# Sketched attention and a gated network on one core: weight columns regrouped for narrowing, the first batch's q handled in pieces, row transfers merged

## The chip, the cores and the metric

The kernel runs on one core of a Trainium2 chip. TensorE (PE in the profile) multiplies matrices, VectorE (DVE), ScalarE (ACT) and GpSimd (POOL) do elementwise work, SyncE (SP) issues most of the transfers, and 16 DMA engines move data between HBM and the on-chip memories: SBUF, and PSUM, where TensorE writes. Each engine runs its own instructions in the order in which they were written, and waits for others by semaphores. The metric is the time of one execution on the device, in microseconds. Lower is better.

## What is computed

```
phi(x) = outer product of (S1 x) and (S2 x), 8 x 8 = 64 features     # S1, S2: 8 x 32
kv  = phi(k)^T v ;  z = sum over the sequence of phi(k)
num = phi(q) kv  ;  den = phi(q) z + 1e-6
attn = num / den                       # 4 batches, 4 heads, 1088 positions, 32 per head
x = attn as (4 * 1088, 128)            # the heads side by side
out = (sigmoid(x w_gate) * (x w_val)) w_out     # w_gate, w_val: 128 x 1536, w_out: 1536 x 128
```

All of it is float32, but S1, S2 and the three weights arrive as float64. [...]the kernel reads them as pairs of 32-bit words and builds float32 values from the pair on the chip. The text calls this narrowing.

## The kernel before

**The network.** The 4352 tokens are cut into eight chunks of 512 and one of 256, and the 1536 hidden columns into NJ = 12 blocks of 128, numbered j. `w1` (line 345) does one wave: x times the gate block and x times the value block into a PSUM tile `wave`, a sigmoid on ScalarE into `sg` (line 365), and, by the `glu` that it leaves behind, the product `g` on VectorE (line 381). `w2` (line 307) multiplies a `g` with the block of w_out and accumulates in `moeout`, which lies in one of two PSUM banks, acc0 for even chunks and acc1 for odd ones. `slot(group, waves)` (line 395) runs a piece of other work and then so many waves; within each wave it first does the pending `glu`, then a `w2` that lies two waves back, then `w1`. The engines' order is exactly this order of calls.

**The attention.** For batch 0 it runs ahead of the network and delivers the tokens in two pieces: 512 tokens (n = 0) before the first wave, 576 tokens (n = 1) during the first chunk. `turn_q` (line 430) transposes q on VectorE, `qcomp` (line 593) multiplies it by the sketch (`cqps`) and copies the result to `cq`, `spread` (line 617) writes `cq` to a scratch tensor `dq` in HBM and reads it back with every row repeated, into `qp` and `bq`, and `qmult` (line 653) multiplies the two to the features of q. `dn` (line 835) makes the denominators (`dps`), the numerators (`nps`), and divides them into `xT`. Batches 1 to 3 are worked on between waves by the loop at line 1035.

**Narrowing.** `narrow` (line 83) is a generator with four steps. Step 0 clamps the high words into `cap` on GpSimd (line 97) and scales the low words into `tail` on ScalarE (line 101). Step 1 shifts and masks `cap` into `head` in two instructions on VectorE (lines 105 and 109). Step 2 squares `cap` on ScalarE (line 117) and adds `tail` to `head` on GpSimd (line 118). Step 3 multiplies `head` with a test on the square on VectorE, into the weight tile `w_sb` (line 127). The square goes to a PSUM bank if one is named, else back over `cap`.

The blocks 0 and 1 are narrowed by `narrow_01` in three parts: gate and value of block 0, gate and value of block 1, and w_out of both (256 columns each). From block 2 on `narrow_w(j, step)` takes gate, value and w_out of block j together (384 columns), one block per wave of the first chunk, in the lines that `w1` runs when `ci == 0`:

```
            if 0 < j0 < NJ - 2:
                narrow_w(j0 + 1, 3)
            narrow_w(j0 + 2, 1)
            narrow_w(j0 + 2, 2)
```

Their squares lie in bank acc1, except for blocks 10 and 11, which have none. The `dps` of piece n = 1 lies in acc1 as well.

**The order of the first chunk** is written out by hand: wave 0; wave 1; `turn_q(0, 1)` between waves 1 and 2; wave 2; then `q01` (`qcomp` and `spread` for piece 1) and waves 3 to 8; `qmult(0, 1)` in one instruction; `load_kq(1)`, which loads k and q of batch 1 into the buffer that `bq` held; wave 9; `part(0, 1)`, that is the pending `glu` and `dn(0, 1)`, with the last step of block 11 inside its division; waves 10 and 11.

**The transfers.** SP issues in this order: S1, S2, the first part of q, gate and value of block 0, v, gate and value of block 1, w_out of blocks 0 and 1, the rest of q, and then pair by pair gate, value and w_out of two blocks. `spread` makes four row transfers for each piece: for each half c of the partitions, one into `qp` and one into `bq`, 64 partitions each.

Of the kernel before, what the change touches and what calls it, by code (L numbers as in the profile page):

```python
# [9 lines left out]
I32 = mybir.dt.int32  # L10
# [10 lines left out]
def kernel(  # L21
# [32 lines left out]
    sbA = ctx.enter_context(tc.tile_pool(name="sbA", bufs=2))  # L54
    raw = ctx.enter_context(tc.tile_pool(name="raw", bufs=NJ // 2))
    sbN = ctx.enter_context(tc.tile_pool(name="sbN", bufs=1))
# [26 lines left out]
    def narrow(out, bits, eng, bank=None, copies=None):  # L83
# [7 lines left out]
        def tmp(dt, tag, bufs):  # L91
# [15 lines left out]
            op0=ALU.logical_shift_left, op1=ALU.bitwise_and,  # L107
        )
        nc.vector.scalar_tensor_tensor(  # L109
            out=head, in0=cap, scalar=-0x40000000, in1=head, op0=ALU.bitwise_and, op1=ALU.bitwise_or  # L110
# [33 lines left out]

    w_sb = const.tile([P, 3, NJ, P], F32, tag="w_sb", name="w_sb")
    w_in = {}

    def load_w_in(j0, j1):
        cs = slice(j0 * P, j1 * P)
        n, jj = divmod(j0, 2)  # L150
        if wide and jj == 0:
            w_in[n] = raw.tile([P, 3, 2, P, 2], I32, tag="w_in", name="w_in")
        for i, src in enumerate((moe_w_gate, moe_w_val)):
            if wide:
                nc.sync.dma_start(
                    out=w_in[n][:, i, jj : jj + j1 - j0].rearrange("p j m w -> p (j m w)"),
                    in_=src[:, cs].bitcast(I32),
                )
            else:
                nc.sync.dma_start(  # L160
                    out=w_sb[:, i, j0:j1].rearrange("p j m -> p (j m)"), in_=src[:, cs]
                )

    def load_w_out(n):
        j0, j1 = 2 * n, 2 * n + 2
        cs = slice(j0 * P, j1 * P)
        src = moe_w_out[cs, :].bitcast(I32) if wide else moe_w_out[cs, :]
        nc.sync.dma_start(
            out=w_in[n][:, 2].rearrange("p j m w -> p j (m w)") if wide else w_sb[:, 2, j0:j1],
            in_=src.rearrange("(j p) m -> p j m", p=P),  # L170
        )

    narrowing = {}

    def narrow_w(j, step):
        if not 0 <= j < NJ:
            return
        n, jj = divmod(j, 2)
        if wide:
            if step == 0:  # L180
                narrowing[j] = narrow(
                    w_sb[:, :, j, :], w_in[n][:, :, jj], nc.gpsimd, "acc1" if j < NJ - 2 else None
                )
            next(narrowing[j])


    def narrow_01(part, step):
        if wide:
            if step == 0:
                i = (slice(0, 2), part) if part < 2 else (2, slice(0, 2))  # L190
                narrowing["01", part] = narrow(
                    w_sb[:, i[0], i[1]],
                    w_in[0][:, i[0], i[1]],
                    nc.gpsimd,
                    "acc0" if part else "acc1",
                )
            next(narrowing["01", part])

# [46 lines left out]
    load_w_in(1, 2)  # L245
    load_w_out(0)
    load_rows(q, 0, q_t[0], ((T0, T, nc.sync),))
    for n in range(1, NJ // 2):
        load_w_in(2 * n, 2 * n + 2)
        load_w_out(n)  # L250

# [55 lines left out]
    def w2(ci, j0, jn, g):  # L307
# [4 lines left out]
        for jj in range(jn):  # L312
            j = j0 + jj
            nc.tensor.matmul(  # L314
                out=moe["acc"][:, :tw],
                lhsT=w_sb[:, 2, j, :],
                rhs=g[:, jj, :tw],
                start=(j == 0),
                stop=(j == NJ - 1),
            )  # L320
        if j0 + jn == NJ:
# [6 lines left out]
            while c < t0 + tw:  # L328
# [14 lines left out]
                c += n * 32  # L343

    def w1():

# [7 lines left out]
        for o in range(0, tw, tp):  # L354
            for which in range(2):
                for jj in range(jn):
                    nc.tensor.matmul(  # L357
                        out=wv[:, which, jj * tw + o : jj * tw + o + tp],
                        lhsT=w_sb[:, which, j0 + jj, :],
                        rhs=xT[:, t0 + o : t0 + o + tp],  # L360
                        start=True,
                        stop=True,
                    )
        sg = sbG.tile([P, TCH], F32, tag="sg", name="sg", bufs=3)
        nc.scalar.activation(out=sg, in_=wv[:, 0], func=ACTF.Sigmoid)  # L365
        if ci == 0:
            if j0 == 1:
                narrow_01(2, 3)
            if 0 < j0 < NJ - 2:
                narrow_w(j0 + 1, 3)  # L370
            narrow_w(j0 + 2, 1)
            narrow_w(j0 + 2, 2)
            if j0 < 3:
                narrow_w(j0 + 3, 0)
            if j0 > 1:
                narrow_w(j0 + 4, 0)

# [51 lines left out]

    def turn_q(b, n):  # L430
        if b >= B:
            return
        if n == 0:
            qT_of[b] = sbA.tile([P, TP, 2, 32], F32, tag="qT", name="qT", bufs=1)
        t0, tn = q_chk[n]
        nc.vector.transpose(  # L436
            out=qT_of[b][:, t0 : t0 + tn].rearrange("p t c s -> p (t c s)"),
# [179 lines left out]
    def spread(b, ns, cq, put, get):  # L617
# [3 lines left out]
        for n in ns:  # L621
            for c in range(2):
                for i, t in enumerate((QP[b], BQ[b])):
                    d0 = d[64 * n + 32 * c + 2 * i, 0]
                    rows = [[8 * W1, R], [0, R]] if i == 0 else [[0, R], [8 * W1, R]]
                    get.dma_start(  # L626
                        out=t[64 * c : 64 * c + 64, n * H * W1 : (n + 1) * H * W1],
                        in_=bass.AP(
                            tensor=d0.tensor, offset=d0.offset, ap=rows + [[1, H * W1]]
                        ),  # L630
                    )

        if len(ns) < 2:
# [18 lines left out]

    def qmult(b, n):
        q0 = half(QP[b], n)
        nc.vector.tensor_tensor(out=q0, in0=q0, in1=half(BQ[b], n), op=MUL)  # L655

# [38 lines left out]
    def kvd(b):  # L695
        KVD[b] = sbA.tile([P, 2, 2, F], F32, tag="kvd", name="kvd")
        k0 = KVZ[b][:, : 2 * F]
# [209 lines left out]
    if wide:  # L907
        steps = narrow(s4, s_in, nc.vector, copies=4)
        for _ in range(3):
            next(steps)  # L910
# [54 lines left out]
    for pi in range(2):  # L965
        outer(0, pi, NJK - 1, NJK, eng=nc.gpsimd)
    for part in range(2):
        narrow_01(part, 0)
    spread_z()
# [8 lines left out]
    def rest(turn, rc, dT):  # L978
# [7 lines left out]
        kvd(0)  # L986
        narrow_01(0, 1)
        narrow_01(0, 2)
        ndt(0)
# [4 lines left out]
    def head1():  # L994
        narrow_01(1, 1)
        narrow_01(0, 3)
        narrow_01(1, 2)
        narrow_01(2, 0)
        narrow_w(2, 0)

    divide((0, 4), (4, 8), between=head1)
    narrow_01(1, 3)
    narrow_01(2, 1)
    narrow_01(2, 2)

# [11 lines left out]

    def part(b, n, between=None):
        glu()
        dn(b, n)(between=between)  # L1020

# [3 lines left out]

    slot(None, 1)
    turn_q(0, 1)
    slot(None, 1)
    slot(q01, 6)
    qmult(0, 1)  # L1030
    load_kq(1)
    slot(None, 1)
    slot(lambda: part(0, 1, lambda: narrow_w(NJ - 1, 3)), 2)
    v_t[1] = load_v(1)
    for b in range(1, B):
        more = b + 1 < B
        wn = 1 if b == 1 else 2
        turn_k(b)
        turn_q(b, 0)
        slot(None, wn)  # L1040
        turn_q(b, 1)
        slot(lambda: begin(b), 1)
        for pi in range(2):
# [50 lines left out]
```

## Time and profile before

| | |
|---|---|
| median of 6 runs | 304.6 us (304.46 to 305.35) |
| the profiled execution | 304.56 us, of which 302.8 us from the first to the last instruction (the span) |
| clock that was granted to TensorE | 0.997 of full |
| weight DMAs: gate, value | 256 KB each for two blocks, 5.8 and 4.8 us from issue to landing |
| weight DMAs: w_out | 256 KB for two blocks, 7.1 us |
| row DMAs of batches 1 to 3, `qp` and `bq` | 288 KB each, 9.7 and 10.0 us |

The numbers after an "x" are counts. A line of a timeline reads: start from the beginning of the span, length, engine, line of the code, operation, what is written and what is read, shape, and in brackets how long the engine stood idle ahead of it and who ended that. "PEld" is TensorE's loading of weights, which runs beside its products. A matrix product of float32 appears as two records for each instruction.

### The profile page before, as it was taken

To read this page: it belongs to the slowest core of one execution; us is meant where nothing else is said; L and a number is where in the kernel's file an instruction comes from. 1 tells how busy PE (TensorE), PEld (TensorE's weight loads), DVE (VectorE), ACT (ScalarE), POOL (GpSimd) and SP (SyncE) were. 2 spreads that over 40 slices of the span, in tenths; PEclk is the share of its full clock that TensorE was granted. 3 is DMA by queue.
4 is the path that set the end of the run, shared out by engine and by line. 5 is a ranking of instruction groups with operands and counts; after the bars stand their busy time and mean duration, and the time that the engine had idled before them with its cause. 6 is when DMAs were issued, how large, how long until landed. Compare 5 with 4: busy or idle time off the path is not lost.

```text
span 302.8 us, 3657 instructions
## 1 busy us (share of the span) xinstructions
PE 296.0 (98%) x1363; PEld 136.3 (45%) x1363; DVE 154.6 (51%) x268; ACT 80.7 (27%) x150; POOL 36.3 (12%) x68
## 2 busy tenths in 40 slices
PE   8899999999999999999999999999999999999995
PEld 3444433443444444434444444444444444444683
DVE  6997788774645554364465541744232223222331
ACT  3556532222122222221222222221222222222220
POOL 1465540610000400000002300000000000000000
PEclk9999999999999999999999999999999999999998
DMA  7993440797201493360013990200010000100011
GB/s 218 350 343 74 124 141 8 169 211 182 93 10 24 110 216 69 72 191 1 0 20 79 173 156 4 36 2 0 0 26 8 0 0 10 27 0 0 8 30 17
DMA packets 31410, 24.24 MB, mean 80 GB/s; under 512 B 21344, under 2 KB 26592, under 8 KB 31392
## 3 DMA queue, kind: packets, MB, share of 16 engines
q1 hardware_dynamic: 27024, 16.15, 20.5%
q0 software_dynamic: 3456, 7.09, 12.1%
q10 hardware_dynamic: 912, 0.77, 0.9%
q8 instruction: 11, 0.18, 0.3%
q14 instruction: 7, 0.06, 0.1%
HBM read 20.73 MB, written 3.26 MB: 79 GB/s over the span
## 4 chain that ended last, share of the span: by engine, by line
PE 84%; DMA 7%; DVE 4%; POOL 3%; issue 1%; SPq 1%; ACT 0%; POOLq 0%
PE wave L357 52%; PE moeout L314 27%; DMA v<-in_v_dram 3%; POOL head L118 3%; DMA w_in<-in_moe_w_out_dram 2%; DMA w_in<-in_moe_w_gate_dram 2%; DVE w_sb L127 1%; DVE head L109 1%; PE kvz L677 1%; PE nps L864 1%; DVE head L105 1%; PE kps L456 1%; PE cqps L602 0%; PE denj L798 0%; PE deni L812 0%
## 5 line engine op out<-in xcount | busy, mean ns | idle before, releaser
L357 PE MATMUL wave<-xT,w_sb 128*128 128x512 f32 (+1 forms) x436 | 191.7, 565 | 0.1
L381 DVE TENSOR_TENSOR g<-wave,sg 128x512 f32<-128x512 f32 x102 | 70.3, 690 | 133.4 <-ACT sg L365 133.2
L357 PEld LDWEIGHTS wave<-xT,w_sb 128*128 128x128 f32 x436 | 82.6, 190 | 93.6 <-issue 86.4
L365 ACT ACTIVATE sg<-wave 128x512 f32<-128x512 f32 x102 | 60.9, 597 | 199.0 <-PE wave L357 193.1
L314 PE MATMUL moeout<-g,w_sb 128*128 128x512 f32 (+1 forms) x216 | 105.8, 577 | 0.3 <-DVE w_sb L127 0.3
L314 PEld LDWEIGHTS moeout<-g,w_sb 128*128 128x128 f32 x216 | 39.3, 190 | 44.0 <-issue 37.4
L626 POOL DMA_DIRECT2D qp<-dq x12 | 7.1, 590 | 108.7 <-DMA dq<-cq 68.7
L118 POOL TENSOR_TENSOR head<-head,tail 128x384 int32<-128x384 int32 (+2 forms) x14 | 13.3, 953 | 18.2 <-DVE head L109 15.1
L535 DVE TENSOR_TENSOR kp<-kab 128x1152 f32<-128x1152 f32 (+2 forms) x10 | 10.5, 1070 | 0.0
L655 DVE TENSOR_TENSOR qp<-qp,bq 128x1152 f32<-128x1152 f32 (+1 forms) x7 | 9.0, 1288 | 1.2 <-DMA bq<-dq 1.2
L109 DVE SCALAR_TENSOR_TENSOR head<-cap,head 128x384 int32<-128x384 int32 (+2 forms) x14 | 7.5, 535 | 0.5
L127 DVE SCALAR_TENSOR_TENSOR w_sb<-square,head 128x384 f32<-128x384 f32 (+1 forms) x11 | 5.7, 519 | 3.9 <-POOL head L118 3.9
L258 PE MATMUL warm<-const-float32-1.0 128*128 128x512 f32 (+1 forms) x12 | 6.6, 666 | 0.8 <-PEq L1078 0.8
L626 POOL DMA_DIRECT2D bq<-dq x12 | 6.9, 576 | 0.4 <-issue 0.2
L324 DVE STREAM_TRANSPOSE o_sb<-moeout 128x512 f32<-128x512 f32 (+1 forms) x9 | 6.1, 678 | 1.4 <-PE moeout L314 1.3
L101 ACT ACTIVATE tail<-w_in 128x384 int32<-128x384 uint32 (+1 forms) x13 | 6.6, 522 | 0.5 <-DMA w_in<-in_moe_w_gate_dram 0.5
L97 POOL TENSOR_SCALAR cap<-w_in 128x384 f32<-128x384 f32 (+1 forms) x13 | 6.4, 500 | 0.0
L897 DVE TENSOR_TENSOR xT<-nps,rb 128x576 f32<-128x576 f32 (+2 forms) x9 | 5.9, 661 | 0.7
L864 PE MATMUL nps<-qp,nd 64*32 64x256 f32 (+1 forms) x128 | 5.5, 401 | 0.4 <-ACT nd L741 0.4
L436 DVE STREAM_TRANSPOSE qT<-kq 128x512 f32<-128x512 f32 (+1 forms) x8 | 5.8, 719 | 0.0
L117 ACT ACTIVATE square<-cap 128x384 f32<-128x384 f32 (+1 forms) x11 | 5.1, 464 | 1.8 <-DVE w_sb L127 1.7
L425 DVE STREAM_TRANSPOSE kT<-kq 128x1088 f32<-128x1088 f32 (+2 forms) x5 | 5.3, 1070 | 0.0
(89 smaller groups left out, 85.2 us busy)
## 6 DMA issues: line engine op xcount, KB each, us to landing
qp<-dq POOLq DMA_DIRECT2D x12, 288.0 KB, 9.7
bq<-dq POOLq DMA_DIRECT2D x12, 288.0 KB, 10.0
v<-in_v_dram SPq DMA_DIRECT2D x16, 144.0 KB, 6.4
kq<-in_k_dram SPq DMA_DIRECT2D x3, 544.0 KB, 4.2
kq<-in_q_dram SPq DMA_DIRECT2D x3, 544.0 KB, 5.1
w_in<-in_moe_w_out_dram SPq DMA_DIRECT2D x6, 256.0 KB, 7.1
w_in<-in_moe_w_gate_dram SPq DMA_DIRECT2D x5, 256.0 KB, 5.8
w_in<-in_moe_w_val_dram SPq DMA_DIRECT2D x5, 256.0 KB, 4.8
```

Of the source, the lines that this page charges most:

```text
L101: nc.scalar.activation(out=tail, in_=lo, func=ACTF.Copy, scale=2.0**-29)
L109: nc.vector.scalar_tensor_tensor(out=head, in0=cap, scalar=-0x40000000, in1=head, op0=ALU.bitwise_and, op1=ALU.bitwise_or)
L118: nc.gpsimd.tensor_tensor(out=head, in0=head, in1=tail, op=ALU.add)
L127: nc.vector.scalar_tensor_tensor(out=out, in0=square, scalar=1.265625 * 2.0**-30, in1=head, op0=ALU.is_ge, op1=MUL)
L314: nc.tensor.matmul(out=moe["acc"][:, :tw], lhsT=w_sb[:, 2, j, :], rhs=g[:, jj, :tw], start=(j == 0), stop=(j == NJ - 1),)
L357: nc.tensor.matmul(out=wv[:, which, jj * tw + o : jj * tw + o + tp], lhsT=w_sb[:, which, j0 + jj, :], rhs=xT[:, t0 + o : t0 + o + tp], sta ...
L365: nc.scalar.activation(out=sg, in_=wv[:, 0], func=ACTF.Sigmoid)
L381: nc.vector.tensor_tensor(out=g, in0=wv[:, 1], in1=sg, op=MUL)
L535: eng.tensor_tensor(out=KP[b][:, pi, j0:j1].rearrange("p j m (i l) -> p (j m) i l", i=R), in0=bass.AP(tensor=a0.tensor, offset=a0.offset, ...
L626: get.dma_start(out=t[64 * c : 64 * c + 64, n * H * W1 : (n + 1) * H * W1], in_=bass.AP(tensor=d0.tensor, offset=d0.offset, ap=rows + [[1, ...
L655: nc.vector.tensor_tensor(out=q0, in0=q0, in1=half(BQ[b], n), op=MUL)
L864: nc.tensor.matmul(out=t[32 * h : 32 * h + 32, c, :w], lhsT=ND[b][rows, 32 * h : 32 * h + 32], rhs=half(QP[b], n)[rows, 2 * (h % 2) + h // ...
```

## The change

Five things change.

1. Gate, value and w_out are grouped differently. Alone are now: gate and value of blocks 0, 1 and 2 (256 columns each), and w_out of blocks 0 and 1 (128 columns each). From block 3 on, gate and value of block j go together with w_out of block j - 1 (384 columns), and w_out of block 11 comes alone at the end (128 columns). The weight tile and the tiles of raw words are laid out to suit; the DMAs of w_out are 0, then 1, then 2, then 3 and 4, and so on to 11 alone, one DMA more than before. All squares of blocks 3 to 11 lie in acc1.
2. `narrow` has five steps: the two VectorE instructions of step 1 are steps 1 and 2.
3. q of batch 0, piece 1: its transpose comes in two instructions (320 and 256 wide) in waves 2 and 3, its product in three (288, 576 and 288 wide) in waves 8, 9 and 10. `q01` runs after wave 3 instead of wave 2, and `part(0, 1)` after wave 10 instead of wave 9. The work of batches 1 to 3 shifts by one wave against the network with it; batch 1 has a wave between the transposes of k and of q.
4. The row transfers into `qp` are one for both halves (128 partitions); those into `bq` stay two. This holds for all batches.
5. `kvd` has one buffer instead of two.

```diff
     def narrow(out, bits, eng, bank=None, copies=None):
...
+        yield
         nc.vector.scalar_tensor_tensor(
             out=head, in0=cap, scalar=-0x40000000, in1=head, op0=ALU.bitwise_and, op1=ALU.bitwise_or
         )
...
+    for j in range(NJ if wide else 0):
+        bits = w_in[j // 2][:, :, j % 2]
+        if j < 3:
+            at = slice(j, j + NJ + 1, NJ)
+            places["gv", j] = at, bits[:, :2], f"acc{1 - j % 2}"
+        else:
+            at = slice(j, j + 2 * NJ + 1, NJ)
+            places[j] = at, bits, "acc1"
+    if wide:
+        for j, bank in enumerate(("acc0", None)):
+            places["out", j] = (
+                slice(2 * NJ + 1 + j, 2 * NJ + 2 + j), w_in[j][:, 2, 1 - j : 2 - j], bank
+            )
+        places[NJ] = slice(3 * NJ, 3 * NJ + 1), w_in[NJ // 2][:, 0], None
...
     load_w_in(1, 2)
-    load_w_out(0)
+    load_w_out(0, 1)
+    load_w_out(1, 2)
     load_rows(q, 0, q_t[0], ((T0, T, nc.sync),))
...
     def w1():
...
         if ci == 0:
...
+            if j0 == 0:
+                narrow_w(("gv", 2), 1, 2, 3)
+                narrow_w(("out", 0), 4)
+                narrow_w(3, 0)
+            elif j0 == 1:
+                narrow_w(("gv", 2), 4)
+                narrow_w(("out", 1), 1, 2, 3)
+                narrow_w(3, 1, 2)
+                narrow_w(("out", 1), 4)
+                narrow_w(3, 3)
+                narrow_w(4, 0)
+            else:
+                if j0 in between:
+                    between[j0]()
+                narrow_w(j0 + 1, 4)
+                narrow_w(j0 + 2, 1, 2, 3)
+                if j0 <= 6:
+                    narrow_w(j0 + 3, 0)
+                if j0 >= 6:
+                    narrow_w(j0 + 4, 0)
...
     def spread(b, ns, cq, put, get):
...
-            for c in range(2):
-                for i, t in enumerate((QP[b], BQ[b])):
+            for i, t in enumerate((QP[b], BQ[b])):
+                for c in (0, 1) if i else (0,):
                     d0 = d[64 * n + 32 * c + 2 * i, 0]
-                    rows = [[8 * W1, R], [0, R]] if i == 0 else [[0, R], [8 * W1, R]]
+                    rows = [[0, R], [8 * W1, R]] if i else [[8 * W1, 2 * R], [0, R]]
                     get.dma_start(
-                        out=t[64 * c : 64 * c + 64, n * H * W1 : (n + 1) * H * W1],
+                        out=t[64 * c : 64 * c + 64 if i else P, n * H * W1 : (n + 1) * H * W1],
...
-    slot(None, 1)
-    turn_q(0, 1)
-    slot(None, 1)
-    slot(q01, 6)
-    qmult(0, 1)
+    between.update(
+        {
+            2: lambda: turn_q(0, 1, 0, 5),
+            3: lambda: turn_q(0, 1, 5),
+            8: lambda: qmult(0, 1, 0, 1),
+            9: lambda: qmult(0, 1, 1, 3),
+            10: lambda: qmult(0, 1, 3),
+        }
+    )
+    slot(None, 3)
+    slot(q01, 7)
     load_kq(1)
-    slot(None, 1)
-    slot(lambda: part(0, 1, lambda: narrow_w(NJ - 1, 3)), 2)
+    slot(lambda: part(0, 1), 1)
...
     for b in range(1, B):
...
+        glu()
         turn_k(b)
+        if b == 1:
+            slot(None, 1)
+            glu()
         turn_q(b, 0)
-        slot(None, wn)
+        if b > 1:
+            slot(None, wn)
         turn_q(b, 1)
+        if b == 1:
+            slot(None, wn)
         slot(lambda: begin(b), 1)
```

The head of the program calls the same steps by their new names: of gate and value 0 and 1 in the same places as before, then of w_out 0 alone where w_out of both blocks stood.

## The prediction

> **What bounds the kernel now.** I read the busy table first, then the chain of waits, then the timelines of TensorE, VectorE and GpSimd from 8 to 52 us, then the table of stretches for the transfers.
>
> ```profile
> PE 296.0 (98%) x1363; PEld 136.3 (45%) x1363; DVE 154.6 (51%) x268; ACT 80.7 (27%) x150; POOL 36.3 (12%) x68
> ```
>
> TensorE is the bound, and from 46 us on nothing interrupts it: in the chain of waits a wave (two products of 512 columns) takes 1.72 us and a `moeout` product 0.86 us, back to back to the end. Only the first 46 us have gaps. TensorE's timeline (start, length, engine, line):
>
> ```profile
> 15.16 3.71 PE L357 MATMUL wave<-xT,w_sb 128*128 128x256 f32 x12
> 19.21 1.12 PE L314 MATMUL moeout<-g,w_sb 128*128 128x512 f32 x2 [0.34 <-DVE w_sb L127]
> 20.17 1.88 PE L357 MATMUL wave<-xT,w_sb 128*128 128x512 f32 x4
> 21.98 0.69 PE L602 MATMUL cqps<-qT,skq 64*32 64x288 f32 x8
> ...
> 39.01 1.88 PE L357 MATMUL wave<-xT,w_sb 128*128 128x512 f32 x4
> 40.94 0.69 PE L844 MATMUL dps<-qp,zb 128*32 128x288 f32 x8
> ...
> 43.17 1.88 PE L357 MATMUL wave<-xT,w_sb 128*128 128x512 f32 x4
> 44.88 1.02 PE L314 MATMUL moeout<-g,w_sb 128*128 128x512 f32 x2
> 46.00 1.98 PE L357 MATMUL wave<-xT,w_sb 128*128 128x512 f32 x4
> ```
>
> The modelled end lies 0.16 behind the true one (1.88 against 1.72), so the first two waves end at 18.71. The gaps: 0.50 before 19.21, 0.10 before 20.17, 0.09 before 21.98, 0.21 before 40.94, 0.26 before 46.00. With 0.1 for the wave that follows a stall (46.00 to the next product at 47.82 is 1.82, not 1.72), about 1.3 us is all that could be won.
>
> What sets these gaps is the narrowing of weight column j, a loop over VectorE and GpSimd:
>
> ```profile
> 35.57 0.56 DVE L127 SCALAR_TENSOR_TENSOR w_sb<-square,head 128x384 f32<-128x384 f32 x1 [0.60 <-POOL head L118]
> 36.05 0.35 DVE L105 TENSOR_SCALAR head<-cap 128x384 int32<-128x384 int32 x1
> 36.43 0.56 DVE L109 SCALAR_TENSOR_TENSOR head<-cap,head 128x384 int32<-128x384 int32 x1
> 36.91 0.68 DVE L381 TENSOR_TENSOR g<-wave,sg 128x512 f32<-128x512 f32 x1
> 38.19 0.56 DVE L127 SCALAR_TENSOR_TENSOR w_sb<-square,head 128x384 f32<-128x384 f32 x1 [0.60 <-POOL head L118]
> ...
> 39.53 1.35 DVE L655 TENSOR_TENSOR qp<-qp,bq 128x1152 f32<-128x1152 f32 x1
> ```
>
> ```profile
> 37.16 0.99 POOL L118 TENSOR_TENSOR head<-head,tail 128x384 int32<-128x384 int32 x1 [1.13 <-DVE head L109]
> 38.13 0.53 POOL L97 TENSOR_SCALAR cap<-w_in 128x384 f32<-128x384 f32 x1
> 39.79 1.95 POOL L118 TENSOR_TENSOR head<-head,tail 128x384 int32<-128x384 int32 x1 [1.13 <-DVE head L109]
> ```
>
> One turn is w_sb 0.48, L105 0.38, L109 0.56, 0.17 to GpSimd, head 0.99, 0.04 back: 2.62 us. TensorE's turn is 2.58, so the loop never gains on it: `w_sb` of wave 9 is ready at 38.75, 0.26 before its use. VectorE's 0.60 idle in each turn is the time in which GpSimd makes `head`.
>
> **What the Trainium skill says.** "SBUF — State Buffer", section "Who interferes with whom": GpSimd and VectorE's second port are one exclusive lock; a VectorE instruction with two SBUF inputs, or a `tensor_scalar` in a two-port mode, and a GpSimd instruction that reads SBUF exclude each other for the whole instruction. The trace agrees: the `head` that met L655 took 1.95 instead of 0.99; L105 at 25.23 took 0.68 instead of 0.35 beside two `cap`s; L109 at 17.21 took 1.01 instead of 0.56 beside a `head`. Products `g` (one input in PSUM) and transposes met `head` and left it at 1.00.
>
> "DMA: Bandwidth & Descriptors", section "Why a DMA increments its semaphore by 16 and not by 1": a transfer runs on the largest number of engines up to 16 that divides the outermost dimension of source and target. The old row transfers have 8 rows outermost, hence 8 engines. The trace agrees: in the table of stretches (the last two columns are DMA share and GB/s) they hold half of the engines, where 128-row loads hold all.
>
> ```profile
> 30.00:32.00 2.00, 2.00 (x6) 0.94 (x5) 1.64 (x4) 1.37 (x3) 0.87 (x3) 1.00 0.51 145
> 44.00:45.00 1.00, 1.00 (x4) 0.49 (x3) 0.90 (x4) 0.00 (x0) 0.36 (x1) 1.00 1.01 418
> ```
>
> **The change, part by part.**
>
> *First waves.* Widths of 128 aren't in the trace: linear from 256 and 384, L105 0.20, L109 0.30, w_sb 0.29, head 0.46 (the 16x32 rows, 0.17 to 0.24, bound them below, the 256 rows above). Both kernels stand at w_sb of gate/val 1 at 15.83. Then, in the new order: out 0 on L105/L109 16.16 to 16.70, its head 16.87 to 17.33; L109 of gate/val 2 begins at 16.91, finds the port taken, ends 17.61; w_sb out 0 17.53 to 17.82; g 0 17.83 to 18.51 (its sigmoid ends 17.79 as before); head of gate/val 2 17.78 to 18.51, w_sb 18.55 to 18.97. So `moeout` 0 starts at 18.71 when TensorE is free, not 19.21, and wave 2 at 19.57, not 20.17: 0.60 won. Next out 1 and j 3: L109 of 3 again meets a head and ends 20.45; head 3 20.62 to 21.62; w_sb 3 at 21.66 (before 22.08). The first piece of q, 320 wide, lies in the idle before it. Wave 3 at 22.28, `cqps` (now after wave 3) at 24.06, wave 4 at 25.54; before 26.14. Still 0.60 ahead.
>
> *The loop to wave 8.* Five turns: w_sb 8 at 21.66 + 5 x 2.62 = 34.76, ready before wave 8 (25.54 + 4 x 2.58 = 35.86).
>
> *Wave 9.* `cap` of 9 and 10 are now made together at j0 = 6, as 5 and 6 were before: L105 0.33 late. The product of q comes in pieces of 288, 576, 288, each behind g, that is into the 0.60 idle. But it has two SBUF inputs and `head` is running: it waits for its end. From 256 wide at 0.43 (L711) and 1152 at 1.35, a piece of 288 takes 0.46 and 576 takes 0.76, of which 0.31 and 0.61 follow the release; less the usual overlap of 0.08 and the 0.04, w_sb comes 0.20 or 0.50 later. w_sb 9: 34.76 + 2.62 + 0.33 + 0.20 = 37.91, ready 38.47; wave 9 is due at 38.44 and starts about 38.53.
>
> *Wave 10 and `dps`.* w_sb 10: 37.91 + 2.62 + 0.50 = 41.03, ready 41.59; wave 10 at 41.65 instead of 41.11. w_sb 11: 41.03 + 2.62 + 0.20 = 43.85, ready 44.41. Here is the new wait: `square` of j = 11 lies in bank acc1 (before, 10 and 11 had none), and `dps` takes acc1, in the compiled order behind w_sb 11. Wave 10 ends at 43.37, `dps` starts at 44.47: 1.10 lost. From `dps` to the next wave took 40.94 to 43.17 = 2.23, so wave 11 starts at 46.70. Before: 46.00, with the same TensorE work done. Less 0.10, since wave 11 no longer follows a stall: **+0.60**. Queued behind `dps` are `nps`, `moeout` 9 and wave 11, all of them on the path.
>
> *The rows.* cq waits on ScalarE behind square 5 and tail 6: about 26.8 instead of 24.18, its DMA at 27.5, the gets 2.4 later (24.84 to 27.23 before) at 29.9. Before, the last bytes moved at 36.4, 9.2 after the first issue. Of 144 KB per engine on 8 engines, 108 remain (36 of the 16-engine transfer, 72 of the two others): 8.4 us of moving become 6.3, landing about 37.0. Piece 0 can't run before head 9 ends, about 37.9: hidden with 0.9 to spare.
>
> *No cost.* One more early weight DMA (0.43 of SP's issue): `tail` and `cap` never waited for weights past the first. kvd with one buffer: a batch apart. On POOL's queue each later batch issues six row DMAs instead of eight (0.58 each); on SP's, four output DMAs (0.44 each) now stand ahead of dq of batch 1, but their data is ready 3 us before cq. TensorE has no gap there that either could fill or open. The load of batch 1's k moves from 40.9 to 44.3, lands 4.2 later, and is turned after g 11 at about 49.8. xT of piece 1 is ready near 48, used at 49.3. Everything later keeps its distance, one wave further on.
>
> **Sum.** Profiled execution 304.56 + 0.60 = 305.2 us (span 302.8 to 303.4); the median of the runs, 304.6, is the same within 0.04.
>
> **Rivals.** *The idle does take the pieces* (port time shared after all, the 1.95 something else): w_sb 11 ready at 43.51, `dps` 43.57, wave 11 at 45.80: -0.3, 304.3. Against it: three collisions in the trace. *Faster:* the narrow first steps don't collide either; w_sb 3 at 21.1, no delay at L105, w_sb 11 ready at 42.6, wave 11 at 44.9: -1.2, 303.4. It decides if w_sb 11 is ready by 43.3. *The rows land late:* at the old pace 39.1, 1.1 past the cover; VectorE stands with w_sb 9 and g 8 behind it: wave 11 at 48.1, 306.6. It begins to count at 37.9.
>
> **Numbers.** Forecast 0.52 (its own range 304.8 to 305.8), pieces hidden 0.18, faster 0.14, late rows 0.16. A difference below 0.2%, 0.6 us, counts as none. Slower: half of the forecast's and the late rows, 0.43; faster: the third case and a little of the second, 0.17; same 0.40. Range 303.9 to 306.4: the ends leave out most of the faster case and half of the late one.
>
> **What would show it.** `moeout` 0 without a wait near 18.7; two of the `head`s or pieces at waves 8 to 10 lengthened, VectorE's L655 forms above 0.46 and 0.76; gaps before waves 9 and 10, and about 1.1 us before `dps`, released by w_sb. Wrong would be a `dps` without a gap, or a wait of L655 for a DMA.

## The result, and the profile after

The changed kernel takes 306.4 us (median of 16 runs, 305.54 to 310.78) against 304.68 us for the kernel before (37 runs beside it): a ratio of 1.0043, with a 95% interval of 1.0029 to 1.0057, or about 1.3 us. The ratio leaves out executions that were slow at a lower clock (here the one of 310.78 us, at 0.989) and isn't the quotient of the two medians, which is 1.0056, or 1.7 us. The profiled execution took 306.43 us with a span of 304.6. The change makes the kernel slower, by two to three times the 0.6 us that were forecast.

The busy table still has TensorE as the bound, with one point less of the span:

```profile
PE 296.3 (97%) x1363; PEld 136.2 (45%) x1363; DVE 157.3 (52%) x277; ACT 81.2 (27%) x154; POOL 33.2 (11%) x66
```

TensorE's work has hardly changed (296.0 us before), so most of the 1.8 us by which the span grew are idle time. Its timeline after the change shows where:

```profile
18.66 1.02 PE L328 MATMUL moeout<-g,w_sb 128*128 128x512 f32 x2
19.52 1.88 PE L373 MATMUL wave<-xT,w_sb 128*128 128x512 f32 x4
...
24.17 0.69 PE L630 MATMUL cqps<-qT,skq 64*32 64x288 f32 x8
...
39.26 1.98 PE L373 MATMUL wave<-xT,w_sb 128*128 128x512 f32 x4 [0.47 <-DVE w_sb L128]
...
42.37 1.98 PE L373 MATMUL wave<-xT,w_sb 128*128 128x512 f32 x4 [0.27 <-DVE w_sb L128]
...
45.19 0.69 PE L872 MATMUL dps<-qp,zb 128*32 128x288 f32 x8 [0.83 <-DVE w_sb L128]
...
47.42 1.88 PE L373 MATMUL wave<-xT,w_sb 128*128 128x512 f32 x4
...
79.08 0.48 PE L840 MATMUL deni<-pd,head 128*32 128x160 f32 x8 [0.24 <-DVE pd L834]
```

The start came as forecast: the gap before the first `moeout` is gone. Then four gaps open: before waves 9 and 10, before `dps` of q half 1 (the kernel before lost 0.21 us there), and, in batch 1, before `deni`. The brackets name the releaser: three times a weight block that was narrowed too late (`w_sb`), once the product `pd`. Wave 11 stands at 47.42 instead of 46.00. `deni` of batch 1 comes one wave (2.58) later in the new order; against the kernel before

```profile
74.89 0.48 PE L812 MATMUL deni<-pd,head 128*32 128x160 f32 x8
```

it has lost 79.08 - 74.89 - 2.58 = 1.61 us. From there to the end 0.2 us more were lost, which I didn't trace.

VectorE's timeline shows how the narrowing came to be late (the line numbers have moved: L109 is now L110, L127 is L128, L655 is L683):

```profile
34.98 0.56 DVE L128 SCALAR_TENSOR_TENSOR w_sb<-square,head 128x384 f32<-128x384 f32 x1 [0.61 <-POOL head L119]
35.48 0.68 DVE L105 TENSOR_SCALAR head<-cap 128x384 int32<-128x384 int32 x1
...
38.01 0.73 DVE L683 TENSOR_TENSOR qp<-qp,bq 128x288 f32<-128x288 f32 x1 [0.66 <-DMA bq<-dq]
38.66 0.55 DVE L128 SCALAR_TENSOR_TENSOR w_sb<-square,head 128x384 f32<-128x384 f32 x1
...
40.58 1.27 DVE L683 TENSOR_TENSOR qp<-qp,bq 128x576 f32<-128x576 f32 x1
41.77 0.55 DVE L128 SCALAR_TENSOR_TENSOR w_sb<-square,head 128x384 f32<-128x384 f32 x1
...
43.69 0.97 DVE L683 TENSOR_TENSOR qp<-qp,bq 128x288 f32<-128x288 f32 x1
44.59 0.55 DVE L128 SCALAR_TENSOR_TENSOR w_sb<-square,head 128x384 f32<-128x384 f32 x1
```

And GpSimd's, over the same time:

```profile
36.93 1.00 POOL L119 TENSOR_TENSOR head<-head,tail 128x384 int32<-128x384 int32 x1 [0.99 <-ACT tail L101]
37.89 0.53 POOL L97 TENSOR_SCALAR cap<-w_in 128x384 f32<-128x384 f32 x1
40.24 0.99 POOL L119 TENSOR_TENSOR head<-head,tail 128x384 int32<-128x384 int32 x1 [1.82 <-DVE head L110]
41.20 0.81 POOL L97 TENSOR_SCALAR cap<-w_in 128x128 f32<-128x128 f32 x1
```

Lay the two side by side. The second piece of the product is issued at 40.58, in the middle of the `head` that began at 40.24. It takes 1.27 us, and it ends 0.62 after that `head` does. A product of this size takes an estimated 0.76 us when nothing holds it up (experiment 3). So VectorE stood still for most of the first 0.65 us, and the profile counts this as length of the instruction, not as idle time. The `cap` that follows the `head` then waits for the piece in its turn: 0.81 us for 128 columns, where the same form took 0.29 when nothing was in its way (at 40.57 us in the run of the second experiment).

The first piece had a different misfortune. It waited for its rows until 38.01. In the table of stretches (last columns: clock, DMA share, GB/s) the transfers had been quiet for a microsecond by then:

```profile
36.00:36.50 0.50, 0.50 (x3) 0.21 (x2) 0.47 (x2) 0.50 (x3) 0.00 (x0) 1.00 0.43 147
36.50:37.00 0.50, 0.50 (x3) 0.26 (x2) 0.50 (x2) 0.41 (x1) 0.07 (x1) 1.00 0.36 81
37.00:37.50 0.50, 0.50 (x3) 0.20 (x2) 0.35 (x1) 0.00 (x0) 0.50 (x1) 1.00 0.00 0
```

The last bytes moved shortly before 37.0, when the forecast has them, but the wait ended one microsecond later. By then the `head` was over, and a `cap` had the port.

In batch 1 the loss is on another path. The timeline of all engines from 54 us, and VectorE's later one (`denj`, `pd` and `deni` are steps of the denominators of batch 1):

```profile
55.19 3.48 SPq L349 DMA_DIRECT2D out_dram<-o_sb  x4
...
55.69 0.64 ACT L638 COPY cq<-cqps 128x576 f32<-128x576 f32 x1 [0.60 <-PE cqps L630]
...
58.72 0.50 SPq L648 DMA_DIRECT2D dq<-cq  x1
```

```profile
71.22 1.22 DVE L683 TENSOR_TENSOR qp<-qp,bq 128x1024 f32<-128x1024 f32 x1 [1.21 <-DMA bq<-dq]
...
76.58 1.36 DVE L683 TENSOR_TENSOR qp<-qp,bq 128x1152 f32<-128x1152 f32 x1 [2.28 <-DMA bq<-dq]
77.86 0.68 DVE L408 TENSOR_TENSOR g<-wave,sg 128x512 f32<-128x512 f32 x1
78.46 0.48 DVE L834 TENSOR_TENSOR pd<-denj,a 128x320 f32<-128x320 f32 x1
```

`cq` was made at 56.33, but its DMA `dq` was issued at 58.72, behind the four outputs of the first chunk on SP; in the kernel before, the outputs came after it:

```profile
51.80 0.64 ACT L610 COPY cq<-cqps 128x576 f32<-128x576 f32 x1 [0.60 <-PE cqps L602]
52.46 0.33 SPq L620 DMA_DIRECT2D dq<-cq  x1
53.53 0.87 SPq L335 DMA_DIRECT2D out_dram<-o_sb  x2
```

The rows come late, both products wait for them, `g` and `pd` stand behind the second product on VectorE, and `deni` waits for `pd`.

### The profile page after: what moved, and what is told of

Read it like the earlier page. It is cut to its first block, busy times and chain, and to the rows that moved or that the text cites. A ratio compares the mean times of both kernels' runs of the same rounds, so it can differ in the third digit from the quotient of the medians.

```text
span 304.6 us, 3671 instructions
## 1 busy us (share of the span) xinstructions
PE 296.3 (97%) x1363; PEld 136.2 (45%) x1363; DVE 157.3 (52%) x277; ACT 81.2 (27%) x154; POOL 33.2 (11%) x66
## 4 chain that ended last, share of the span: by engine, by line
PE 90%; DVE 3%; DMA 3%; issue 1%; ACT 1%; SPq 0%; POOL 0%; POOLq 0%; DVEq 0%; ACTq 0%
PE wave L373 55%; PE moeout L328 28%; DMA v<-in_v_dram 2%; PE nps L892 2%; PE kvz L705 1%; DMA s_in<-in_S_dram 1%; PE cqps L630 1%; DVE qp L683 1%; DVE g L408 1%; PE kps L484 1%; DVE w_sb L128 0%; PE dps L872 0%; PE kvz L691 0%; PE deni L840 0%; DVE kT L452 0%
## 5 line engine op out<-in xcount | busy, mean ns | idle before, releaser
L655 POOL DMA_DIRECT2D qp<-dq x6 | 3.5, 584 | 114.3 <-DMA dq<-cq 74.1
L119 POOL TENSOR_TENSOR head<-head,tail 128x384 int32<-128x384 int32 (+3 forms) x16 | 12.8, 799 | 19.8 <-DVE head L110 11.8
L683 DVE TENSOR_TENSOR qp<-qp,bq 128x1024 f32<-128x1024 f32 (+3 forms) x9 | 10.7, 1186 | 4.1 <-DMA bq<-dq 4.1
L110 DVE SCALAR_TENSOR_TENSOR head<-cap,head 128x384 int32<-128x384 int32 (+3 forms) x16 | 7.8, 487 | 0.6
L128 DVE SCALAR_TENSOR_TENSOR w_sb<-square,head 128x384 f32<-128x384 f32 (+2 forms) x13 | 6.5, 501 | 2.7 <-POOL head L119 2.7
L97 POOL TENSOR_SCALAR cap<-w_in 128x384 f32<-128x384 f32 (+2 forms) x15 | 7.3, 497 | 0.0
L101 ACT ACTIVATE tail<-w_in 128x384 int32<-128x384 uint32 (+2 forms) x15 | 6.8, 475 | 0.8 <-DMA w_in<-in_moe_w_out_dram 0.8
L655 POOL DMA_DIRECT2D bq<-dq x12 | 6.7, 576 | 0.3 <-issue 0.2
L118 ACT ACTIVATE square<-cap 128x384 f32<-128x384 f32 (+2 forms) x13 | 5.9, 450 | 2.6 <-DVE w_sb L128 2.5
L464 DVE STREAM_TRANSPOSE qT<-kq 128x512 f32<-128x512 f32 (+3 forms) x9 | 5.8, 658 | 0.0
```

The lines of the kernel that those rows point to most:

```text
L97: eng.tensor_scalar(out=cap.bitcast(F32), in0=hi.bitcast(F32), scalar1=122880.0, scalar2=-122880.0, op0=ALU.min, op1=ALU.max,)
L101: nc.scalar.activation(out=tail, in_=lo, func=ACTF.Copy, scale=2.0**-29)
L110: nc.vector.scalar_tensor_tensor(out=head, in0=cap, scalar=-0x40000000, in1=head, op0=ALU.bitwise_and, op1=ALU.bitwise_or)
L119: nc.gpsimd.tensor_tensor(out=head, in0=head, in1=tail, op=ALU.add)
L655: get.dma_start(out=t[64 * c : 64 * c + 64 if i else P, n * H * W1 : (n + 1) * H * W1], in_=bass.AP(tensor=d0.tensor, offset=d0.offset, ap ...
L683: nc.vector.tensor_tensor(out=q0, in0=q0, in1=b0, op=MUL)
```

## The experiments

**Theory 1.** The loss has two parts. In the head of the kernel the pieces of the q product need the port that GpSimd's `head` and `cap` use; the narrowing loop loses what they wait, and `dps`, which shares a PSUM bank with the square of step 11, waits for the last weight block. In batch 1, `dq` stands behind four outputs. **Rival 1:** the regrouping of the weights costs by itself. **Rival 2:** the merged row transfer is slower or lands later. **Rival 3:** VectorE is simply full, and the port doesn't matter.

Two marks in TensorE's timeline measure each part. Both are counted from the first `dps`, which lies between 10.73 and 11.55 us in these executions: the first loads don't always land at the same time, and all that follows moves with them. Where wave 11 stands (in the new order the first wave after `nps`, in the old order the second) shows the head; how much later `deni` of batch 1 comes shows batch 1. Values of the old order have the one wave of 2.58 added to `deni`.

The labels that begin with x name the runs.

| kernel | median, us | ratio to before, 95% | wave 11 | `deni` | between |
|---|---|---|---|---|---|
| before | 304.6 | | 35.08 | 66.55 | 31.47 |
| after | 306.4 | 1.0043 (1.0029 to 1.0057) | 36.54 | 68.20 | 31.66 |
| x1, square 11 in SBUF | 306.04 | 1.0033 (1.0022 to 1.0043) | 36.03 | 67.39 | 31.36 |
| x2, outputs later | 306.11 | 1.0014 (0.998 to 1.0048) | 36.52 | 67.87 | 31.35 |
| x3, no product | 304.74 | 0.9993 (0.9982 to 1.0003) | 35.12 | 66.56 | 31.44 |
| x4, before with merged rows | 304.67 | 0.9990 (0.9978 to 1.0003) | 35.12 | 66.58 | 31.46 |
| x5, x13, four row transfers | 309.09, 310.56 | 1.0114 (1.0076 to 1.0152), 1.0153 (1.0122 to 1.0183) | x13: 36.87 | 68.64 | 31.77 |
| x6, caps earlier | 306.10 | 1.0037 (1.0024 to 1.0050) | 36.37 | 67.72 | 31.35 |
| x7, product from PSUM | 304.91 | 0.9992 (0.9971 to 1.0013) | 35.16 | 66.51 | 31.35 |
| x12, the same from SBUF | 306.13 | 1.0039 (1.0026 to 1.0053) | 36.14 | 67.52 | 31.38 |
| x11, `dq` by ScalarE | 306.05 | 1.0037 (1.0023 to 1.0050) | 36.51 | 67.86 | 31.35 |
| x8, x7 + x1 + x11 | 304.96 | 0.9992 (0.9980 to 1.0005) | 35.35 | 66.70 | 31.35 |
| x10, x8 with one copy earlier | 304.26 | 0.9984 (0.9977 to 0.9992) | 34.69 | 66.05 | 31.36 |

**1. Take the product away.** This kernel (x3) leaves out the three pieces, so q half 1 keeps only one of its two factors.

```diff
-            8: lambda: qmult(0, 1, 0, 1),
-            9: lambda: qmult(0, 1, 1, 3),
-            10: lambda: qmult(0, 1, 3),
```

> Leaves out the q product of half 1 of batch 0 (its three pieces), so that half keeps only one factor. Theory 1 (the pieces take VectorE time and the port that the narrowing needs): w_sb 9, 10, 11 follow at the turn of about 2.6 us, near 38.0, 40.6, 43.2 us; the gaps before waves 9, 10 and before dps fall to below 0.2 us each; the time falls by 1.1 to 1.4 us, to about 305.0, which is close to the kernel before. Rival 1 (the regrouping into a w_out with the next gate, val costs by itself): the gaps stay and the time falls by less than 0.4 us. Rival 2 (the merged transfer of the rows is late): no product is left that waits for rows, so it also falls by what the wait for them cost, 0.7 us at most.

w_sb 9, 10 and 11 came at 37.84, 40.46 and 43.08 us, the gaps before waves 9 and 10 went, and the time fell by 1.7 us to that of the kernel before, a little more than said. The gap before `dps` stayed at 0.64 us, not below 0.2: `dps` still waits for w_sb 11 through the bank. So rival 1 fails as the reason for the gaps before waves 9 and 10. It doesn't fall altogether here: this kernel has less to do than the kernel before, whose product is whole, and is only as fast, and the bank of the square is part of the regrouping. Experiment 8 settles it. This run can't tell the port from the wait for rows or from VectorE's time.

**2. The product with one operand in PSUM** (x7). ScalarE copies the `b` rows, two heads at a time, into the PSUM tile that is free between `cqps` and `nps`. VectorE multiplies in two pieces in turns 9 and 10.

```diff
-            8: lambda: qmult(0, 1, 0, 1),
-            9: lambda: qmult(0, 1, 1, 3),
-            10: lambda: qmult(0, 1, 3),
+            9: lambda: times_b(0),
+            10: lambda: times_b(2),
         }
     )
+    pair = {}
+    def copy_b(h):
+        t = ps2.tile([P, 2, 512], F32, tag="two", name="bps2")
+        pair[h] = t[:, :, :W1]
+        nc.scalar.copy(out=pair[h], in_=half(BQ[0], 1)[:, h : h + 2])
+    def times_b(h):
+        q0 = half(QP[0], 1)[:, h : h + 2]
+        nc.vector.tensor_tensor(out=q0, in0=q0, in1=pair[h], op=MUL)
+    behind.update({8: lambda: copy_b(0), 9: lambda: copy_b(2)})
```

`behind` is run in `w1` after the narrowing steps of its turn.

> ScalarE copies the b rows of the product into PSUM, two heads at a time, and VectorE multiplies from there in two pieces of 576 columns, in turns 9 and 10, so that each piece reads one operand from SBUF. VectorE's work is the same in sum. Theory 1 (the pieces lose by the shared port): the pieces take about 0.65 us each beside GpSimd's work without stretching it or waiting for it, in time that VectorE stood waiting for head; w_sb 9, 10, 11 come near 37.9, 40.6, 43.3 us, and the time is 1.0 to 1.3 us below the changed kernel, about 305.2. Rival 3 (VectorE itself is full, the port does not matter): w_sb 10 and 11 are still 0.6 us late each, and the time is at most 0.5 us below the changed kernel.

VectorE's timeline of this kernel:

```profile
38.01 0.56 DVE L128 SCALAR_TENSOR_TENSOR w_sb<-square,head 128x384 f32<-128x384 f32 x1 [0.60 <-POOL head L119]
...
39.94 0.75 DVE L1073 TENSOR_TENSOR qp<-qp,bps 128x576 f32<-128x576 f32 x1
40.64 0.56 DVE L128 SCALAR_TENSOR_TENSOR w_sb<-square,head 128x384 f32<-128x384 f32 x1
...
42.57 0.75 DVE L1073 TENSOR_TENSOR qp<-qp,bps 128x576 f32<-128x576 f32 x1
43.26 0.56 DVE L128 SCALAR_TENSOR_TENSOR w_sb<-square,head 128x384 f32<-128x384 f32 x1
```

And GpSimd's:

```profile
39.60 1.00 POOL L119 TENSOR_TENSOR head<-head,tail 128x384 int32<-128x384 int32 x1 [1.13 <-DVE head L110]
40.57 0.29 POOL L97 TENSOR_SCALAR cap<-w_in 128x128 f32<-128x128 f32 x1
```

Each piece lies in what used to be idle, `w_sb` keeps the turn of 2.62 us through it, and `head` and `cap` keep their lengths. The time fell by 1.5 us, back to that of the kernel before. But this run also moved the pieces away from their late rows.

**3. The control: the same pieces, the same copy, but into SBUF** (x12; over raw words of block 0 that are no longer needed).

```diff
-        t = ps2.tile([P, 2, 512], F32, tag="two", name="bps2")
-        pair[h] = t[:, :, :W1]
+        pair[h] = w_in[0].rearrange("p a b m w -> p (a b m w)")[:, : 2 * W1]
+        pair[h] = pair[h].bitcast(F32).rearrange("p (h w) -> p h w", h=2)
```

> The same as the run with the product through PSUM, but ScalarE's copy of the b rows goes to SBUF, so that the same pieces at the same places read two operands from SBUF. Theory 1 (the port): each piece takes 1.2 to 1.4 us instead of 0.75, blocked by GpSimd's head, w_sb 10 is 0.5 to 0.6 us and w_sb 11 1.0 to 1.2 us later than with PSUM, and the time is about 1.0 us above that run. Rival 3 (it was the place of the pieces and the wait for the rows, not the port): the same as with PSUM within 0.2 us.

VectorE's timeline, and below it GpSimd's:

```profile
37.92 0.56 DVE L128 SCALAR_TENSOR_TENSOR w_sb<-square,head 128x384 f32<-128x384 f32 x1 [0.60 <-POOL head L119]
...
39.86 1.28 DVE L1073 TENSOR_TENSOR qp<-qp,w_in 128x576 f32<-128x576 f32 x1
41.06 0.54 DVE L128 SCALAR_TENSOR_TENSOR w_sb<-square,head 128x384 f32<-128x384 f32 x1
...
42.98 1.27 DVE L1073 TENSOR_TENSOR qp<-qp,w_in 128x576 f32<-128x576 f32 x1
44.17 0.54 DVE L128 SCALAR_TENSOR_TENSOR w_sb<-square,head 128x384 f32<-128x384 f32 x1
```

```profile
39.52 1.00 POOL L119 TENSOR_TENSOR head<-head,tail 128x384 int32<-128x384 int32 x1 [1.13 <-DVE head L110]
40.48 0.81 POOL L97 TENSOR_SCALAR cap<-w_in 128x128 f32<-128x128 f32 x1
```

This is the pair to compare: the same place in the order, the same shape, no wait for a DMA in either, and 1.28 us against 0.75 us. The piece is issued 0.34 us into `head` and ends 0.62 after it. Nor is PSUM the quicker source: with both operands in SBUF and GpSimd doing nothing, a product of 288 columns takes 0.46 us (x13, experiment 6) and one of 1024 takes 1.22 (the changed kernel at 71.22 us), which makes an estimated 0.76 for 576. w_sb 10 and 11 are 0.51 and 1.00 us later than from PSUM, once the start of each execution is taken out (0.09). The medians lie 1.2 us apart, and the intervals of the ratios don't meet. Rival 3 falls: where the second operand lies decides whether the piece and GpSimd hold each other up. At wave 11 this is worth 36.14 - 35.16 = 0.98 us; the other 0.40 us up to the changed kernel's 36.54 belong to the place of its three pieces and the wait for the rows, which no run takes apart. It is what the Trainium skill states in "SBUF — State Buffer", section "Who interferes with whom": an instruction of VectorE with at most one SBUF input, outside the two-port modes, doesn't contend with GpSimd, and one with two does when GpSimd's instruction reads SBUF.

**4. `dps` free of the bank of the square** (x1).

```diff
-            places[j] = at, bits, "acc1"
+            places[j] = at, bits, "acc1" if j < NJ - 1 else None
```

> The square of step 11 stays in SBUF, so dps of q half 1 shares no buffer with the narrowing of gate, val 11. Theory 1 (the head loses its time at dps, behind w_sb 11): dps waits only for the last piece of the q product and comes about 0.5 us earlier, near 44.7 us; the gap of 0.83 us before it shrinks to 0.3 to 0.4; the final multiply of step 11 reads one more SBUF operand and may take a little longer. Whole time 0.4 to 0.5 us below the changed kernel, about 305.9. Rival 1 (the grouping of the narrowing itself costs, dps only shows it): wave 11 is then what waits, and the time stays within 0.1 us of the changed kernel.

```profile
44.83 1.11 PE L872 MATMUL dps<-qp,zb 128*32 128x288 f32 x8
```

Wave 11 came 0.51 us earlier on the first mark. What is left of the gap lies within `dps` itself, which took 1.11 instead of 0.69 us, because its last two records wait for the last piece (0.28 us on TensorE's weight loads, released by `qp` at 45.26). The medians differ by 0.4 us, but the two intervals overlap, so the size rests on the trace.

**5. Batch 1: the order on SP, and another queue.** x2 issues the outputs of the first chunk after `spread` in the program; x11 lets ScalarE issue `dq` of batch 1.

```diff
-        put.dma_start(out=d[p0:], in_=cq[p0:])
+        (nc.scalar if b == 1 else put).dma_start(out=d[p0:], in_=cq[p0:])
```

> The four output DMAs of the first token chunk are issued after the transfers of batch 1's q components instead of before. Theory 1: the DMA dq of batch 1 starts at about 56.4 us instead of 58.7, the row transfers land 2.3 us earlier, the first q product of batch 1 no longer waits, and the gap of 0.24 us before deni goes; whole time 0.3 us below the changed kernel, about 306.1. Rival 1 (nothing is lost after the head): no change.

> The changed kernel with the DMA dq of batch 1 issued by ScalarE alone. Theory 1 (batch 1 loses 0.3 us because dq stands behind four outputs): dq at about 56.3 us instead of 58.7, the first q product of batch 1 starts right behind its g, no gap before deni; 0.2 to 0.3 us below the changed kernel. If nothing is lost in batch 1: the same time as the changed kernel.

In x2 the queue of SP didn't follow the order of the calls: two of the four outputs still stood ahead, and `dq` went at 57.54, not at 56.4. (The kernel fixes the order of the calls for PE, VectorE, ScalarE and GpSimd by `manual_schedule`; SP isn't among them.) The first product of batch 1 no longer waited, the second still did, by 1.20 us. In x11 it went at 56.29, and neither product waited (ScalarE's timeline):

```profile
55.62 0.64 ACT L638 COPY cq<-cqps 128x576 f32<-128x576 f32 x1 [0.60 <-PE cqps L630]
56.29 0.34 ACTq L648 DMA_DIRECT2D dq<-cq  x1
```

In both, the stretch from wave 11 to `deni` fell from 31.66 to 31.35, by 0.31 us, with the head unchanged (36.52 and 36.51 against 36.54). But x1, x6, x7 and x12 have 31.35 to 31.38 as well, with `dq` still behind the four outputs. What sets the stretch shows when the runs are laid side by side. When the second product of batch 1 starts more than about 28.85 us after wave 11, `deni` has to wait for it and comes 2.50 us after its start (76.58 to 79.08; in x3, x12 and x13 2.51). When it starts earlier, the stretch is 31.35. In the changed kernel it started 29.16 us after wave 11, in x13 29.26, in x3 28.93, in x12 28.87, in the other runs of the table with the new order between 26.80 and 28.39, and just the first four have a stretch above 31.36. From the issue of `dq` to that product, where it waited for rows of the merged transfers, it took between 16.9 and 18.5 us. So the late `dq` takes away the reserve (it went 11.30 us after wave 11, in x11 8.93), and the single execution decides whether up to 0.3 us are lost. The medians of x2 and x11 lie 0.3 us below the changed kernel's, which is no more than those of x6 and can't be told from noise.

**6. Merged rows: added to the kernel before, taken from the kernel after.** x4 is the kernel before with only the row transfer changed; x5 and x13 are the changed kernel with the old four transfers of 64 rows.

> The kernel before, with only the q rows of both halves in one transfer of 128 rows for each n. Theory 1: no cost and no gain, within 0.2 us of the kernel before. Rival 2 (the merged transfer lands later or hinders the others): slower by 0.3 us or more, with a gap before dps of half 1 or before the products of a later batch.

> The changed kernel with the q rows again in transfers of 64 rows, four for half 1 of batch 0 and eight for the later batches. Theory 1 (the size of the transfer isn't what costs, but piece 0 is at the mercy of when the last rows land): the last of four transfers is issued about 0.6 us later, piece 0 starts 0.4 to 0.8 us later than its 38.0 us, w_sb 9 to 11 follow, and the time is 0.2 to 0.8 us above the changed kernel. Rival 2 (the merged transfer is slower than two of half the rows): the rows land earlier than 37.0 us, piece 0 doesn't wait, and the time is 0.3 us or more below the changed kernel.

> The four-transfer version once more, since its profiled execution ran at a lower TensorE clock from 40 us on and so did not show where 2.7 us go. Theory 1: piece 0 at 39.8 us again (1.8 us later than in the changed kernel), dps 1.6 to 1.8 us later, and the rest of the 2.7 us in batch 1, where eight transfers of 64 rows are issued by GpSimd behind a dq that is itself late: a gap of 0.5 to 1.0 us before deni. Otherwise, if dps is 1.7 us later and deni no more than that, the remaining 1 us is not in the head and not in batch 1.

x4 equals the kernel before, so the merged transfer costs nothing where nothing waits for it. Going back to four transfers in the changed kernel costs more than either theory said: 0.7 and 1.1% by the ratios (1.0114 and 1.0153 against 1.0043), 2.2 and 3.4 us. Rival 2 falls. In the profile of x13 piece 0 started at 39.18 instead of 38.01, 0.60 us later once the start of each execution is taken out (0.57), as its rows came later. No instruction of GpSimd was then in its way, and it took 0.46 us:

```profile
39.18 0.46 DVE L683 TENSOR_TENSOR qp<-qp,bq 128x288 f32<-128x288 f32 x1 [1.23 <-DMA bq<-dq]
```

But this profile, of one of the fastest runs of x13 (307.57), lost only 0.33 us at wave 11 and 0.1 us more by `deni` against the changed kernel, so neither half of the forecast for x13 came true; the runs that its ratio counts spread up to 312 us. The profile of x5 is of an execution of 314.63 us. In it TensorE stood idle for 1.09 of the 2 us from 38 us on, the clock that it was granted from 40 to 45 us was 0.71, and the second product of batch 1 waited 5.31 us for its rows, with a gap of 3.97 us before `deni`. That tells where this one execution lost time, not why the version varies. The cause stays open.

**7. Caps one turn ahead** (x6).

```diff
-                if j0 <= 6:
-                    narrow_w(j0 + 3, 0)
-                if j0 >= 6:
-                    narrow_w(j0 + 4, 0)
+                if j0 == 2:
+                    narrow_w(5, 0)
+                narrow_w(j0 + 4, 0)
```

> The clamp of step j is made one turn earlier from step 6 on (two of them in turn 2 instead of in turn 6). Theory 1: L105 no longer waits for a clamp made just before it, the turn of the loop falls from 2.67 to about 2.62 us over turns 3 to 6, w_sb 8 comes 0.2 to 0.3 us earlier, and piece 0, which waits for its rows, takes part of that back: time 0.1 to 0.3 us below the changed kernel. Rival 1: the turn stays at 2.67, no change.

The turns did fall to 2.61 to 2.63 us, but the turn in which two caps stand together took 3.00 (24.98 to 27.98): its price of 0.33 had only moved from turn 6 forward. w_sb 8 came 0.19 later, not earlier, and w_sb 9 0.17 earlier, which is also what wave 11 gained. The time is within the noise of the changed kernel.

**8. All that helped, together** (x8).

> The product through PSUM as in the run before, the square of step 11 in SBUF, and the DMA dq of batch 1 issued by ScalarE, which made its data, instead of by SP behind the outputs. Theory 1: the three losses add and all go: dps of q half 1 at 43.5 to 43.9 us, dq of batch 1 at about 55 us, no gap before deni; the time is 1.6 to 2.0 us below the changed kernel, about 304.5, which is 0.1 to 0.5 us below the kernel before. Rival 1 (the regrouping costs by itself): it stays 0.5 us or more above the kernel before.

This missed its mark: 304.96 us, no faster than x7. Without a bank the square of step 11 goes back over `cap`, so ScalarE has to wait until VectorE has read `cap` (0.85 us idle before the square). The copy of the second pair stood behind that square, the second piece waited 0.59 us for the copy, and `dps` waited for the piece. x10 has the copy ahead of the square:

```diff
-            9: lambda: times_b(0),
+            9: lambda: (times_b(0), copy_b(2)),
...
-    behind.update({8: lambda: copy_b(0), 9: lambda: copy_b(2)})
+    behind.update({8: lambda: copy_b(0)})
```

> As the run with all three changes, but ScalarE copies the second pair of b rows before the square of step 11, not after it, so that the second piece does not wait for the copy. Theory 1: the second piece starts about 1.2 us after the first w_sb behind it, at 42.5 to 42.6 us, dps of q half 1 starts when wave 10 and its moeout end, 0.5 to 0.6 us earlier than with the product through PSUM alone; 0.4 to 0.6 us below that run and as much below the kernel before, about 304.5. Against it: if another wait takes the place of dps's, it stays within 0.2 us of the kernel before.

TensorE's timeline of x10, and the table of stretches (the first columns: length, PE busy):

```profile
41.33 1.96 PE L374 MATMUL wave<-xT,w_sb 128*128 128x512 f32 x4
43.22 0.83 PE L875 MATMUL dps<-qp,zb 128*32 128x288 f32 x8
...
45.58 1.88 PE L374 MATMUL wave<-xT,w_sb 128*128 128x512 f32 x4
```

```profile
15.00:52.00 37.00, 37.00 (x116) 15.92 (x116) 31.76 (x68) 19.17 (x40) 16.93 (x27) 1.00 0.46 143
52.00:84.00 32.00, 32.00 (x224) 13.70 (x222) 20.16 (x35) 7.74 (x14) 4.63 (x10) 1.00 0.64 155
```

The table shows TensorE busy all the time from 15 to 84 us, where the changed kernel had 35.43 of 37 and 31.76 of 32, and the kernel before 36.52 and 32.00. The median is 304.26 us against 304.71 for the kernel before beside it: 0.45 us, 0.08 to 0.23% faster. This kernel has the regrouped weights and its whole product, so rival 1 falls, and neither the one buffer of `kvd` nor the later order of the batches costs anything that shows. The idea of the change, an earlier first `moeout` and the product in VectorE's idle time, wins something together with the three repairs. How much of it is the regrouping isn't shown: no run has the kernel before with its product from PSUM.

## Why the prediction was right, and where it was short

The direction and the mechanism of the head were right; the size was short by three terms. The measured 306.4 us lies above the forecast's own range (304.8 to 305.8) and at the very end of the whole one, close to the 306.6 of the rival with late rows. That nearness is chance: wave 11 stood at 47.42, not at that rival's 48.1, and the rest was lost in batch 1, where no loss was expected. And one of the two signs that the prediction named for being wrong did appear, the wait of L655 (now L683) for a DMA, beside all the signs for being right.

- *First waves:* right to a few hundredths up to w_sb 3. `moeout` 0 at 18.66 (said: 18.71), wave 2 at 19.52 (19.57), w_sb 3 at 21.64 (21.66). Then `cqps` came at 24.17 (24.06) and wave 4 at 25.75 (25.54), so TensorE was 0.39 us ahead of the kernel before there, not 0.60. It cost nothing, since wave 9 waits for w_sb 9.
- *The loop to wave 8:* said 2.62 us a turn, was 2.67, because each `cap` now runs just ahead of the L105 that needs it; x6, with caps a turn ahead, has 2.61 to 2.63. w_sb 8 at 34.98 instead of 34.76: **0.22 short**.
- *The double cap:* L105 took 0.68 as said.
- *The rows:* the landing near 37.0 was right by luck. `cq` was copied at 25.95 (said: 26.8) and the first transfer issued at 28.97 (29.9), 0.9 us earlier; from there to the last bytes it took 8.0 us where the prediction had 7.1.
- *Piece 0:* the term of +0.20 failed. It was sized for a piece that waits for the end of `head`, with the rows there "0.9 to spare". The last bytes did come by 37.0, but the release came a microsecond later, at 38.01; `head` was over, the port belonged to the next `cap`, and the piece took 0.73. From w_sb 8 to 9 it was 3.68 us instead of 3.15: **0.53 short**. So the rival with late rows, which was to count from 37.9 on, had set in by 0.1 us.
- *Pieces 1 and 2:* said +0.50 and +0.20, turns of 3.12 and 2.82; the trace has 3.11 and 2.82. The price of a collision, worked out from the lengths of two products in the trace before (256 and 1152 columns), held: the pieces of 576 and 288 columns ended 0.62 and 0.32 us after `head`, said were 0.61 and 0.31.
- *`dps`:* said to wait for acc1 until 44.47; it waited until 45.19, later by 0.72, which is the 0.22 + 0.53 of the two terms above to 0.03. x1 shows that the bank was worth 0.51 us.
- *"No cost":* wrong for SP. The prediction saw the four outputs ahead of `dq` of batch 1, but called their data ready 3 us before `cq`. `o_sb` was ready at 55.16, behind the transpose of q on VectorE, 1.2 us before `cq`, and four issues took 3.48 us, 0.87 each where the prediction had 0.44. **0.31 short** in this execution; others with the same order on SP and the same transfers lost 0 to 0.1 (experiment 5).

Together: 0.60 forecast + 0.72 at `dps` + 0.31 in batch 1 = 1.63, and 1.61 was measured at `deni`, all in the profiled execution.

## What to carry to other kernels

Idle time of VectorE beside a busy GpSimd wasn't free here for products with two SBUF inputs (1.28 us), and was for the same products with one in PSUM (0.75). Before filling such time, add up what both engines do with the port, and try one operand in PSUM if the sum is full. When work is moved, count from the release of the wait for a DMA and not from its last byte (0.7 to 1.1 us later in these runs), and look at what then stands ahead on the issuing queue, with the time of each issue. Where two tiles share a bank by name, as `dps` and the square of step 11 do, look there for the next wait (0.51 us here).

## What was not expected of the hardware

The wait for the rows ended 1.0 us after the last bytes that the trace shows (37.0 and 38.01), in other runs 0.7 to 1.1 after them (in x13 no bytes moved after 38.5, and the piece started at 39.18). In these traces an instruction that is held up at the port appears as a longer instruction, up to 1.28 us instead of 0.75, and not as a wait. The four transfers of 64 rows instead of three left the time not only longer but far less steady (307.5 to 312 us in x13, 305.5 to 306.9 in the changed kernel), which these runs don't explain.
